# Moving 48 additions from GpSimd to VectorE's read of PSUM, and 36 key casts from VectorE to ScalarE, in an attention and mixer kernel

## Chip, cores, metric

One Trainium2 chip, one core. The metric is device time in microseconds (us). Medians are quoted with their range and number of runs. A ratio is the mean time of one kernel's fast runs over that of the other's of the same rounds, so it is not quite the ratio of the quoted medians; its 95% interval stands in brackets. "Faster" or "slower" means by over 2%.

## The reference

```python
# q, k, v: (B=8, H=8, S=1024, D=64); E, F: (64, 1024)
k_proj = einsum('ks,bhsd->bhkd', E, k);  v_proj = einsum('ks,bhsd->bhkd', F, v)
attn = softmax(q @ k_proj^T / sqrt(D));  x = (attn @ v_proj), heads joined   # (8, 1024, 512)
h = maximum(x^T @ w_tok1, 0) @ w_tok2                  # 1024 -> 256 -> 1024
u = x + h^T
out = u + maximum(u @ w_ch1, 0) @ w_ch2                # 512 -> 1536 -> 512
```

The last line is what the change touches: the sum of u and the down-projection's result.

## The kernel before

A small planner in the kernel puts every engine's instructions into one fixed order, from estimated durations; so changing an instruction's engine also changes TensorE's order. Up- and down-projection use a seven-product scheme (as in Strassen's), with sums of blocks on VectorE. The bf16 sums of this scheme (S and G below) have both inputs in SBUF:

```python
def s_sums(j):                       # four sums of 128x512 bf16 before the up-projection ("S", L677)
    one(0, a21, a22, add=True);  one(2, a11, a21)
    one(1, St[:, 0], a11, deps=(0,));  one(3, a12, St[:, 1], deps=(1,))
...
# at the end of up_set: four sums of 128x512 bf16 before the down-projection ("G", L842)
total(3, g21, G[:, 2, cs], True, [q21, g(2)]);  total(5, G[:, 0, cs], g21, False, [q21, g(0)])
total(4, G[:, 3, cs], G[:, 0, cs], False, [g(3), g(0)]);  total(6, G[:, 1, cs], G[:, 4, cs], False, [g(1), g(4)])
```

The down-projection, one of 16 blocks. Banks x, y, z collect products. Before the change ScalarE copies a bank to SBUF and GpSimd adds u there:

```python
def copy_add(dst, key, src, sh, dh):
    act(512, lambda: nc.scalar.copy(out=dst, in_=view(src)), writes=[key], uses=[bk[src]])
    pool(512, lambda: nc.gpsimd.tensor_add(out=dst, in0=dst, in1=u_of(sh, dh)),
         reads=u_key(sh), writes=[key])

product(1, 0)
act(512, lambda: nc.scalar.copy(out=view("y"), in_=view("x")), takes=[bk["y"]], uses=[bk["x"]])
product(7, 1); product(6, 2)
copy_add(db, "db", "y", 1, 0)
product(2, 3)
copy_add(o_of(0, 0), o_key(0, 0), "x", 0, 0)
product(5, 4)
dve(512, lambda: nc.vector.tensor_add(out=da, in0=view("y"), in1=u_of(1, 1)), ...)
dve(512, lambda: nc.vector.tensor_add(out=o_of(1, 1), in0=view("z"), in1=da), ...)
product(3, 5)
copy_add(o_of(0, 1), o_key(0, 1), "y", 0, 1)
store(0)
product(4, 6)
dve(512, lambda: nc.vector.tensor_add(out=o_of(1, 0), in0=view("z"), in1=db), ...)
store(1)
```

Loads and DMA transposes take turns by explicit dependencies. This becomes important below:

```python
def load_kv(b):                                   # k and v of one batch, issued by GpSimd
    last = load_group(b, "kv", turned_u.get((b - 2, 0)))   # behind an older u transpose
    if (b - 2, 1) in turned_u:
        tie(turned_u[b - 2, 1], last)
```

The softmax here doesn't subtract the row's maximum and nothing guards it: scores larger than these inputs give would overflow.

## Time and profile before

| | us |
|---|---|
| time, median of the runs before the prediction | 442.85 (441.47 to 443.28, 3 runs) |
| time of the profiled execution | 440.64 |
| span of the profile | 438.8 |
| TensorE busy, 50 to 400 us | 341.1 of 350 |

The second row is one to keep in mind: the profiled execution was faster than each of the timed runs. The prediction shows the engine line, the stretches, the longest stop and the groups. One part that it only mentions is the end. This is the timeline of the profile before (start, duration in us, engine, line, operation; in brackets the idle time before it and what ended that):

```profile
431.77 1.47 PE L902 MATMUL ps<-wT,G 128*128 128x256 bf16 x12
...
432.63 1.15 POOL L936 TENSOR_TENSOR o<-o,u 128x512 f32<-128x512 f32 x1 [2.89 <-ACT o L934]
433.35 0.69 DVE L964 TENSOR_TENSOR o<-ps,db 128x512 f32<-128x512 f32 x1 [2.16 <-PE ps L902]
433.81 0.84 SPq L929 DMA_DIRECT2D out_dram<-o  x2
```

Read it from below: both last stores (x2) are issued together at 433.81, because the first of them waits for a GpSimd add that lasts to 433.78, although the other half of what it stores was ready by 428.63.

### The profile page before, as it was taken

The page shows a single profiled execution, that of the slowest core. Times are in us where ns is not written, and L with a number is a line of the kernel's source. Part 1 is how long each engine was busy: PE and PEld are TensorE (multiplying, and loading weights), DVE is VectorE, ACT ScalarE, POOL GpSimd, SP SyncE. Part 2 cuts the span into 40 slices and gives each one's busy share as a digit, 9 for nine tenths or more (in the row PEclk, how much of TensorE's full clock was granted, in tenths as well). Part 3 has the DMA queues.
Part 4 walks back from the last instruction along what each step waited for, and adds up shares of the span by engine and source line. Part 5 has one row for each costly group of instructions (what it writes and reads, how often), then busy time and mean ns, then how long its engine had stood idle before and what let it go on. Part 6 is the DMA issues. An engine that isn't in the chain of part 4 may idle for free.

```text
span 438.8 us, 9331 instructions
## 1 busy us (share of the span) xinstructions
PE 417.0 (95%) x3726; PEld 336.1 (77%) x3754; DVE 323.8 (74%) x782; ACT 242.2 (55%) x440; POOL 124.7 (28%) x152
## 2 busy tenths in 40 slices
PE   7899999999999999999999899999999999999993
PEld 3587888576787778787878778787778878888883
DVE  2579969578788868888688868879687876867451
ACT  2758784275456544665457544575447653555530
POOL 8543243150142321422142310523212120223222
PEclk9999999999999999999999999999999999999998
DMA  9999999569799786978339894397830403151122
GB/s 166 207 200 206 206 206 220 97 105 228 132 149 197 167 167 140 175 185 151 120 54 208 160 154 143 61 237 125 179 74 19 128 0 121 26 145 45 53 97 96
DMA packets 89515, 60.89 MB, mean 139 GB/s; under 512 B 55680, under 2 KB 84864, under 8 KB 89472
## 3 DMA queue, kind: packets, MB, share of 16 engines
q0 software_dynamic: 34944, 45.09, 51.7%
q1 hardware_dynamic: 54448, 14.95, 19.8%
q8 instruction: 29, 0.48, 0.4%
q10 hardware_dynamic: 80, 0.26, 0.3%
q14 instruction: 14, 0.11, 0.1%
HBM read 59.24 MB, written 16.78 MB: 173 GB/s over the span
## 4 chain that ended last, share of the span: by engine, by line
PE 74%; DVE 12%; DMA 9%; ACT 2%; issue 1%; POOL 0%; DVEq 0%; ACTq 0%
PE ps L902 27%; PE ps L807 25%; DMA v_sb<-in_v_dram 6%; PE ps L617 5%; PE ps L637 5%; DVE S L677 3%; PE ps L465 3%; DMA uT<-u 3%; PE ps L586 2%; DVE G L842 2%; PE ps L563 2%; PE ps L387 2%; DVE x_sb L603 2%; DVE g L788 1%; DVE u L648 1%
## 5 line engine op out<-in xcount | busy, mean ns | idle before, releaser
L902 PEld LDWEIGHTS <-G 128*128 128x128 bf16 x1344 | 130.2, 98 | 26.6 <-issue 4.4
L902 PE MATMUL ps<-wc_sb,G 128*128 128x256 bf16 x768 | 104.1, 273 | 2.4 <-DVE da L952 1.6
L829 ACT ACTIVATE G<-ps 128x512 bf16<-128x512 f32 x96 | 57.4, 600 | 58.5 <-PE ps L807 58.3
L807 PEld LDWEIGHTS <-wc_sb 128*128 128x128 bf16 x768 | 73.1, 98 | 15.3 <-issue 2.0
L902 PE MATMUL ps<-wT,G 128*128 128x256 bf16 x576 | 78.2, 273 | 1.0 <-DVE o L956 1.0
L936 POOL TENSOR_TENSOR o<-o,u 128x512 f32<-128x512 f32 x32 | 39.1, 1221 | 102.9 <-ACT o L934 98.3
L807 PEld LDWEIGHTS <-wT 128*128 128x128 bf16 x576 | 55.2, 98 | 15.3 <-issue 4.3
L807 PE MATMUL ps<-S,wc_sb 128*128 128x256 bf16 x384 | 57.6, 273 | 0.3
L807 PE MATMUL ps<-uT,wc_sb 128*128 128x256 bf16 x384 | 57.6, 273 | 0.1
L807 PE MATMUL ps<-S,wT 128*128 128x256 bf16 x384 | 55.6, 273 | 0.2 <-DVE S L677 0.2
L788 DVE CUSTOM_DVE_ANT_0 g<-ps,ub 128x512 bf16<-128x512 f32 x48 | 32.7, 682 | 24.9 <-PE ps L807 24.8
L603 DVE TENSOR_TENSOR x_sb<-ps,rdn 128x256 bf16<-128x256 f32 x128 | 50.4, 416 | 0.5
L842 DVE TENSOR_TENSOR G<-G 128x512 bf16<-128x512 bf16 x96 | 45.4, 476 | 3.4 <-DVE G L842 0.5
L936 POOL TENSOR_TENSOR db<-db,u 128x512 f32<-128x512 f32 x16 | 18.7, 1166 | 98.9 <-ACT db L934 98.9
L648 DVE TENSOR_TENSOR u<-ps,x_sb 128x512 bf16<-128x512 f32 x56 | 37.9, 686 | 10.6 <-PE ps L637 6.7
L788 DVE CUSTOM_DVE_ANT_0 G<-ps,ua 128x512 bf16<-128x512 f32 x48 | 32.9, 686 | 14.0 <-ACT ua L835 12.9
L572 ACT ACTIVATE a<-ps 128x512 bf16<-128x512 f32 x64 | 37.3, 603 | 10.1 <-PE ps L563 9.1
L835 ACT COPY ua<-ps 128x512 f32<-128x512 f32 x48 | 28.2, 587 | 21.5 <-PE ps L807 20.8
L835 ACT COPY ub<-ps 128x512 f32<-128x512 f32 x48 | 28.1, 586 | 10.1 <-PE ps L807 10.1
L807 PE MATMUL ps<-uT,wT 128*128 128x256 bf16 x192 | 28.8, 272 | 3.4 <-DVE G L788 3.1
L586 PE MATMUL ps<-vb,a 128*128 128x130 bf16 x256 | 30.1, 220 | 1.5 <-DVE x_sb L603 1.1
L934 ACT COPY o<-ps 128x512 f32<-128x512 f32 x32 | 18.8, 587 | 21.6 <-PE ps L902 21.3
(70 smaller groups left out, 548.9 us busy)
## 6 DMA issues: line engine op xcount, KB each, us to landing
out_dram<-o POOLq DMA_DIRECT2D x30, 512.0 KB, 4.9
k_sb<-in_k_dram POOLq DMA_DIRECT2D x14, 512.0 KB, 7.5
v_sb<-in_v_dram POOLq DMA_DIRECT2D x14, 512.0 KB, 11.9
q_sb<-in_q_dram POOLq DMA_DIRECT2D x14, 512.0 KB, 7.7
wc_sb<-in_moe_w_ch_dram POOLq DMA_DIRECT2D x6, 256.0 KB, 12.4
wc_sb<-in_moe_w_ch_dram POOLq DMA_DIRECT2D x4, 384.0 KB, 12.6
k_sb<-in_k_dram POOLq DMA_DIRECT2D x4, 256.0 KB, 6.8
v_sb<-in_v_dram POOLq DMA_DIRECT2D x4, 256.0 KB, 7.4
```

Of the source, the lines that this page charges most:

```text
L572: lambda: nc.scalar.activation(out=a_t[h % 4], in_=bank(bk), func=ACT.Exp, scale=scale),
L586: nc.tensor.matmul(view()[:, 2 * jj : 2 * jj + 2].rearrange("p c d -> p (c d)"), a_t[h % 4][:, j * P : (j + 1) * P], vb[:, h].rearrange("k ...
L603: lambda: nc.vector.tensor_tensor(out=x_sb[:, 4 * half : 4 * half + 4, h * D : (h + 1) * D], in0=view()[:, :, 0:D], in1=rdn[:, :, None].to ...
L617: nc.tensor.matmul(bank(bk), wt1_sb[:, si, t * P : (t + 1) * P], x_sb[:, si, :], start=(si == 0), stop=(si == NSI - 1),)
L648: lambda: nc.vector.tensor_add(out=u_t[b % 2][:, si, :], in0=bank(bk), in1=x_sb[:, si, :]),
L788: nc.vector._custom_dve(TENSOR_ADD_SAT, out=out, in0=in0, in1=in1, s0=FMAX, s1=0.0)
L807: nc.tensor.matmul(t[:, c, :], w1_of(n, dd, 2 * m + c), a_of(j, n, dd), start=(n in (1, 7) and c == 0 and dd == 0), stop=(c == 1 and dd == 1),
L829: lambda: nc.scalar.activation(out=G[:, n, cs], in_=view(src), func=ACT.Relu),
L835: 512, lambda: nc.scalar.copy(out=dst, in_=view("y")), writes=[(name, s % 2)],
L842: 512, lambda: f(out=G[:, n, cs], in0=in0, in1=in1), ps=False, reads=deps,
L902: nc.tensor.matmul(view(X_OF[n])[:, t, :], G[:, G_OF[n], cc, t * P : (t + 1) * P], w2_of(n, cc), start=(n in (1, 7) and t == 0 and cc == 0 ...
L936: 512, lambda: nc.gpsimd.tensor_add(out=dst, in0=dst, in1=u_of(sh, dh)),
```

## The change

The intent: GpSimd adds nothing any more; VectorE adds u in the pass in which it reads PSUM anyway. In exchange ScalarE, relieved of 48 copies, takes VectorE's casts of the projected and turned keys. The diff, cut to its core:

```diff
-            lambda: nc.vector.tensor_copy(out=kp[:, hs, 0, :], in_=view()[0:KP, 0:hn]),
-            lambda: nc.vector.tensor_copy(out=kp[:, hs, 1, :], in_=view()[0:KP, 0:hn]),
+            lambda: nc.scalar.copy(out=kp[:, hs, 0, :], in_=view()[0:KP, 0:hn]),
+            lambda: nc.scalar.copy(out=kp[:, hs, 1, :], in_=view()[0:KP, 0:hn]),
 ...
-        dve(
-            hn * KP, lambda: nc.vector.tensor_copy(out=kT[0:D, hs, 0, :], in_=view()[0:D, 0:hn]),
+        act(
+            hn * KP, lambda: nc.scalar.copy(out=kT[0:D, hs, 0, :], in_=view()[0:D, 0:hn]),
 ...
-        def copy_add(dst, key, src, sh, dh):
-            act(512, lambda: nc.scalar.copy(out=dst, in_=view(src)), writes=[key], uses=[bk[src]])
-            pool(
-                512, lambda: nc.gpsimd.tensor_add(out=dst, in0=dst, in1=u_of(sh, dh)),
-                reads=u_key(sh), writes=[key],
+        def add_u(dst, key, src, sh, dh):
+            dve(
+                512, lambda: nc.vector.tensor_add(out=dst, in0=view(src), in1=u_of(sh, dh)),
+                reads=u_key(sh), writes=[key], uses=[bk[src]],
             )
 ... (the three calls of copy_add become calls of add_u)
```

More of the change, by code (lines that the diff above doesn't have):

```diff
@@ L307, in act @@
         return pl.add("ACT", t, t + 0.105, fn, **kw)
-    def pool(cols, fn, **kw):
-        t = cols / 512 * 1.15
-        return pl.add("POOL", t, t, fn, **kw)
     def sp(t, fn, **kw):
@@ L486, in kv_proj @@
         ]
-        dve(cols, e[0], writes=[("kp", 0, h) for h in heads], uses=[bk])
-        dve(cols, e[1], writes=[("kp", 1, h) for h in heads], uses=[bk])
+        act(cols, e[0], writes=[("kp", 0, h) for h in heads], uses=[bk])
+        act(cols, e[1], writes=[("kp", 1, h) for h in heads], uses=[bk])
         act(cols, e[2], writes=[("vb", 1, h) for h in heads], uses=[bk])
@@ L946, in down_block @@
         product(6, 2)
-        copy_add(db, "db", "y", 1, 0)
+        add_u(db, "db", "y", 1, 0)
         product(2, 3)
-        copy_add(o_of(0, 0), o_key(0, 0), "x", 0, 0)
+        add_u(o_of(0, 0), o_key(0, 0), "x", 0, 0)
         product(5, 4)
@@ L959, in down_block @@
         product(3, 5)
-        copy_add(o_of(0, 1), o_key(0, 1), "y", 0, 1)
+        add_u(o_of(0, 1), o_key(0, 1), "y", 0, 1)
         store(0)
```

## The prediction

> **What bounds the kernel now.** I read the engine line of the page first, then a table of busy time by stretches of 50 us, then the timeline where TensorE stops, then the groups by shape, then the waits.
>
> The page's engine line (busy us, share of the span, instructions):
>
> ```profile
> PE 417.0 (95%) x3726; PEld 336.1 (77%) x3754; DVE 323.8 (74%) x782; ACT 242.2 (55%) x440; POOL 124.7 (28%) x152
> ```
>
> The table by stretches (us, then busy time and count of PE, PEld, DVE, ACT, POOL):
>
> ```profile
> 100.00:150.00 50.00, 47.91 (x414) 38.09 (x415) 41.45 (x102) 29.13 (x54) 11.76 (x14) 1.00 0.99 181
> 200.00:250.00 50.00, 49.79 (x438) 40.50 (x440) 38.43 (x94) 28.59 (x53) 12.68 (x16) 1.00 0.69 134
> 250.00:300.00 50.00, 47.40 (x409) 38.01 (x411) 38.59 (x89) 27.02 (x49) 11.90 (x14) 1.00 0.80 147
> ```
>
> TensorE is the bound. Busy time alone would not prove it, but the timeline has groups of six 256-column matmuls that follow each other after 0.65 us, 0.108 us each, so the stream is dense and not just overlapping. From 50 to 400 us it is busy 341.1 us of 350. The change touches no matmul of the computation, so it can only win from the remaining 8.9 us there, and from start and end. That is already a ceiling: 442.85 - 8.9 = 434, which is a gain of 2.0%.
>
> Where TensorE stops is therefore the whole question. The longest stop is at 250 us, and the timeline around it (start, us, engine, line) shows the cause:
>
> ```profile
> 248.65 3.40 DVE L677 TENSOR_TENSOR S<-uT 128x512 bf16<-128x512 bf16 x1
> ...
> 249.47 1.18 POOL L936 TENSOR_TENSOR db<-db,u 128x512 f32<-128x512 f32 x1
> ...
> 250.59 1.16 POOL L936 TENSOR_TENSOR o<-o,u 128x512 f32<-128x512 f32 x1
> 251.97 0.68 DVE L788 CUSTOM_DVE_ANT_0 G<-ps,ua 128x512 bf16<-128x512 f32 x1
> ...
> 252.70 0.49 PE L807 MATMUL ps<-uT,wT 128*128 128x256 bf16 x3 [2.37 <-DVE G L788]
> ```
>
> One VectorE subtraction takes 3.40 us and ends 0.29 us after the second GpSimd add ends. [...] the next reader of PSUM (L788) starts only then, and TensorE sits 2.37 us. What the same instruction costs undisturbed is in the groups by shape (count, busy us, mean ns):
>
> ```profile
> L842 DVE TENSOR_TENSOR G<-G 128x512 bf16<-128x512 bf16 x96 | 45.4, 476 | 3.4 <-DVE G L842 0.5
> L842 DVE TENSOR_TENSOR G<-G,g 128x512 bf16<-128x512 bf16 x48 | 20.0, 416 | 0.1
> L677 DVE TENSOR_TENSOR S<-uT 128x512 bf16<-128x512 bf16 x32 | 16.2, 535 | 2.4 <-DMA uT<-u 2.4
> L648 DVE TENSOR_TENSOR u<-ps,x_sb 128x512 bf16<-128x512 f32 x56 | 37.9, 686 | 10.6 <-PE ps L637 6.7 <-PE ps L807 3.6
> L936 POOL TENSOR_TENSOR o<-o,u 128x512 f32<-128x512 f32 x32 | 39.1, 1221 | 102.9 <-ACT o L934 98.3 <-DMA uT<-u 4.5
> L936 POOL TENSOR_TENSOR db<-db,u 128x512 f32<-128x512 f32 x16 | 18.7, 1166 | 98.9 <-ACT db L934 98.9
> ```
>
> I went through all 256 bf16 sums of L677 and L842 in the trace. Sixteen take over 500 ns, every one overlaps a GpSimd add, and they end about 0.3 us after one; together they are 14.0 us longer than 16 x 0.417. The 60 that overlap only GpSimd's issue of a DMA average 415 ns, the 163 that overlap neither 417: no effect of the issues. L648, with one input in PSUM, shows none either (686 ns, longest 693).
>
> [...] the trace has 686 ns for 512 columns, and the new adds have this form. [...] The trace shows the turns for the projected keys and values:
>
> ```profile
> ACT vb L485 <- DVE kp L480: 10.5, 8, 2.0
> DVE kp L481 <- ACT vb L485: 3.7, 8, 0.7
> ```
>
> **The change part by part.**
> - GpSimd: 48 adds go, 39.1 + 18.7 = 57.8 us; 124.7 becomes 66.9, all of it DMA issue and start-up. [...]
> - ScalarE: the 48 copies go, 18.8 + 9.4 = 28.2 us. In come the key casts at the durations of its own value casts: 18 of 64x512 at 0.587, 6 of 64x256 at 0.372, 12 of 64x128 at 0.263: 10.6 + 2.2 + 3.2 = 16.0. 242.2 - 28.2 + 16.0 = 230.
> - VectorE: in come 48 adds of PSUM + u (one SBUF input) at 0.686, 32.9 us. Out go the key casts, 12.0 (kp) + 5.9 (kT) = 17.9, and the 14.0 of held time. 323.8 + 32.9 - 17.9 - 14.0 = 324.8: the load is unchanged, but without pieces of 1 to 3.4 us that nothing planned for.
> - TensorE's path: the stops that follow a held sum are 0.68 at 134.8 us, 0.31 at 146.4, 0.75 at 180.6, 0.36 at 199.0, 2.37 at 252.7 and 0.82 at 305.6, in all 5.3 us. They go: **-5.3**. The other three named stops between 50 and 400 us are 0.23, 0.95 (a VectorE reader behind four u sums and a key cast, at 90.3) and 0.94 (the v load, at 106.6). That load is issued behind a GpSimd add that itself was held to 2.22 us; without it it goes out 1 to 2 us sooner. I count half: **-0.5**.
> - Costs. The static order of TensorE's instructions gains two filler matmuls in the start-up, where the plan expects idle: five took 1.19 us, so **+0.5**. There ScalarE takes 12 more short casts in a phase in which it is on the chain of waits (exps and query copies), but two handoffs of some 0.3 us per head pair vanish; I call it even. New waits of TensorE on VectorE's reads of PSUM: the existing read of the same kind, da, held TensorE in mid-run once in 15 blocks (0.75, behind a held sum), so its undisturbed rate is nil; with three times as many such reads I allow **+1.0**. The last block keeps its two stops (0.72 on db, 0.85 on da): the order is the same, and 0.69 on VectorE stands where 0.59 on ScalarE stood.
> - Sum: 442.85 - 5.3 - 0.5 + 0.5 + 1.0 = **438.5 us**.
>
> **The rivals.**
> (a) VectorE becomes the late engine. It is at 83% in the stretch from 100 to 150 us and each such stretch takes six more adds, 4.1 us, that stand between two products into the same bank, where ScalarE read promptly before. If each of 16 blocks then stopped TensorE by 0.75 us as at 180.6, that is +12 - 5.3, about 449. Against it: three key casts (2.0 us) and 1.8 us of held time leave the same stretch, and VectorE's own idle waits for TensorE (24.8 us at L788) show slack.
> (b) Nothing moves: TensorE's stops close, and reordered work opens as many; 442 to 443. For it: a fifth of TensorE's instructions change place in the static order. Against it: stops without a held sum are rare now, 2.1 us in 350.
> (c) The start-up gets longer by the ScalarE casts: 12 x 0.26 = 3.2 us on the chain at worst, giving 441.5 with the rest as above. For it: ScalarE waits little between 10 and 30 us. Against it: only half of those casts stand before the exps, and the wait for VectorE's casts goes.
> (d) All of the mid-run idle goes and loads come sooner: 434 to 435. It needs every stop closed and none opened.
>
> **Range and chances.** The main term is 5.3 us with its cause seen in each case, so a gain is likely; (b) and (c) pull up, (d) down. 8 in 10: 435 to 443. Faster by over 2% needs below 434.0, beyond the ceiling of the mid-run idle: 0.04. Slower by over 2% needs (a) at more than its price, above 451.7: 0.03. Within 2%: 0.93.
>
> **What would show it.** Right: L677 and L842 at 410 to 420 ns in every group with none over 500; VectorE near 325 us busy, ScalarE near 230, GpSimd near 67; the new adds near 686 ns; TensorE's stop at 250 us gone, and named stops between 50 and 400 us of 2 to 3 us in place of 7.4. Wrong: bf16 sums still stretched[...]; stops of TensorE whose releaser is one of the new adds or a VectorE reader behind them, more than 3 us in all (rival a); first up-projections of the second batch over 1 us later than before (rival c); the same total of stops under other names (rival b).

## The result, and the profile after

| | before | after |
|---|---|---|
| time, median of 4 runs | 442.38 (441.47 to 443.28) | 431.83 (431.61 to 432.40) |
| profile: its own run / span | 440.64 / 438.8 | 431.61 / 429.8 |
| TensorE busy, 50 to 400 us | 341.1 | 347.6 |
| start of the last matmul to the end of the span | 5.87 | 4.70 |

The ratio is 0.9763 [0.9739, 0.9788]: **faster**, by 10.5 us, where 4.3 were predicted, and below the range.

Line numbers moved: L902 is now L898, L807 is L803, L842 is L838, L677 is L673, L788 is L784, L952 is L947, L964 is L959; the new adds are L931. The engine line of the page after:

```profile
PE 415.9 (97%) x3727; PEld 336.2 (78%) x3756; DVE 321.9 (75%) x794; ACT 231.1 (54%) x428; POOL 66.3 (15%) x104
```

The same stretches (us; then busy time and count of PE, PEld, DVE, ACT, POOL; granted clock, DMA share, GB/s) of the profile after:

```profile
100.00:150.00 50.00, 48.66 (x416) 38.75 (x419) 38.80 (x100) 27.20 (x50) 7.61 (x11) 1.00 0.89 157
200.00:250.00 50.00, 49.84 (x437) 40.69 (x440) 38.84 (x98) 27.66 (x49) 6.73 (x10) 1.00 0.81 148
250.00:300.00 50.00, 49.74 (x427) 39.73 (x431) 39.64 (x100) 27.04 (x48) 6.73 (x10) 1.00 0.81 151
```

The stretch from 250 us gained most: TensorE 49.74 in place of 47.40. The groups by shape (count, then busy us, mean ns of one, idle before) of the profile after:

```profile
L838 DVE TENSOR_TENSOR G<-G 128x512 bf16<-128x512 bf16 x96 | 39.8, 417 | 2.5
...
L673 DVE TENSOR_TENSOR S<-uT 128x512 bf16<-128x512 bf16 x32 | 12.4, 412 | 5.2 <-DMA uT<-u 5.2
...
L931 DVE TENSOR_TENSOR o<-ps,u 128x512 f32<-128x512 f32 x32 | 21.9, 685 | 10.2 <-PE ps L898 9.9
L931 DVE TENSOR_TENSOR db<-ps,u 128x512 f32<-128x512 f32 x16 | 10.8, 677 | 0.0
```

The means of 476 and 535 ns became 417 and 412; no bf16 sum takes over 427 ns.

Waits of TensorE on the new adds and on reads like them (total us, times, longest) in the profile after:

```profile
PE ps L898 <- DVE da L947: 1.5, 2, 0.8
...
PE ps L898 <- DVE db L931: 0.8, 1, 0.8
...
PE ps L582 <- DVE x_sb L599: 0.3, 1, 0.3
```

One `da` wait and the `db` wait lie in the last block. In mid-run there remain one `da` wait of 0.71 at 126.7 us and 0.34 at 145.9. The line `PE ps L807 <- DVE G L788: 3.1, 2, 2.4` of before has no counterpart. And the end:

```profile
423.93 1.47 PE L898 MATMUL ps<-wT,G 128*128 128x256 bf16 x12
424.13 0.69 DVE L931 TENSOR_TENSOR o<-ps,u 128x512 f32<-128x512 f32 x1 [0.83 <-PE ps L898]
424.85 1.65 SPq L925 DMA_DIRECT2D out_dram<-o  x2
425.44 0.69 DVE L959 TENSOR_TENSOR o<-ps,db 128x512 f32<-128x512 f32 x1 [0.62 <-PE ps L898]
```

The first store now goes at 424.85, beside the last matmuls and before VectorE's last add; the second follows that add.

**Where the 10.55 us came from, by the traces.** The two profiled spans differ by 9.0: 6.4 more TensorE busy time between 50 and 400 us, 0.2 in the first 50 us, 1.2 in the tail. The rest, 1.2, is less busy time over the same number of matmul records (3726 and 3727), and most likely belongs to the stops as well: pool_fill below, which has the order of before and as many records, is 1.1 us less busy too. Matched one by one, seven matmuls make up that difference. In before each of them starts behind a stop or a short pause (at 134.8, 146.4, 199.0, 252.7, 253.4, 305.6 and 351.7 us) and adds 0.16 us more busy time than in pool_fill, where it overlaps the matmul in front. So in these traces, whose matmul ends are modelled, such a stop costs 0.16 us beyond its idle time. For after, whose order differs, this matching was not possible. The other 1.5 is not in these two profiles: the profiled run of before was 1.74 faster than its median, that of after 0.22 faster than its own.

### The profile page after: what moved, and what is told of

It is laid out like the page before. It is cut to its first block, busy times and chain, and to the rows that moved or that the text cites. A ratio compares the mean times of both kernels' runs of the same rounds, so it can differ in the third digit from the quotient of the medians.

```text
span 429.8 us, 9229 instructions
## 1 busy us (share of the span) xinstructions
PE 415.9 (97%) x3727; PEld 336.2 (78%) x3756; DVE 321.9 (75%) x794; ACT 231.1 (54%) x428; POOL 66.3 (15%) x104
## 4 chain that ended last, share of the span: by engine, by line
PE 86%; DMA 6%; DVE 4%; ACT 2%; issue 1%; DVEq 0%
PE ps L898 31%; PE ps L803 31%; PE ps L613 6%; PE ps L633 4%; DMA v_sb<-in_v_dram 3%; PE ps L582 3%; DMA uT<-u 3%; PE ps L461 3%; PE ps L559 3%; PE ps L383 1%; DVE u L644 1%; PE ps L691 1%; PE ps L718 1%; PE ps L543 1%; ACT qT L551 1%
## 5 line engine op out<-in xcount | busy, mean ns | idle before, releaser
L898 PEld LDWEIGHTS <-G 128*128 128x128 bf16 x1344 | 129.9, 98 | 25.1 <-issue 2.8
L898 PE MATMUL ps<-wc_sb,G 128*128 128x256 bf16 x768 | 104.1, 273 | 2.3 <-DVE da L947 1.5
L803 PEld LDWEIGHTS <-wc_sb 128*128 128x128 bf16 x768 | 73.2, 98 | 16.3 <-issue 2.4
L898 PE MATMUL ps<-wT,G 128*128 128x256 bf16 x576 | 78.2, 273 | 0.0
L803 PEld LDWEIGHTS <-wT 128*128 128x128 bf16 x576 | 55.2, 98 | 12.3 <-issue 1.2
L803 PE MATMUL ps<-S,wc_sb 128*128 128x256 bf16 x384 | 57.7, 273 | 0.3
L803 PE MATMUL ps<-uT,wc_sb 128*128 128x256 bf16 x384 | 57.8, 273 | 0.1
L803 PE MATMUL ps<-S,wT 128*128 128x256 bf16 x384 | 55.7, 273 | 0.4 <-DVE S L673 0.4
L784 DVE CUSTOM_DVE_ANT_0 g<-ps,ub 128x512 bf16<-128x512 f32 x48 | 32.8, 682 | 29.3 <-PE ps L803 29.3
L925 POOL DMA_DIRECT2D out_dram<-o x30 | 16.4, 545 | 192.8 <-DVE o L931 130.8
L838 DVE TENSOR_TENSOR G<-G 128x512 bf16<-128x512 bf16 x96 | 39.8, 417 | 2.5
L784 DVE CUSTOM_DVE_ANT_0 G<-ps,ua 128x512 bf16<-128x512 f32 x48 | 32.8, 683 | 8.2 <-ACT ua L831 7.7
L844 ACT COPY ps<-ps 128x512 f32<-128x512 f32 x48 | 27.7, 577 | 17.1 <-DVE o L931 7.6
L594 DVE RECIPROCAL rdn<-ps 128x4 f32<-128x4 f32 x128 | 20.7, 173 | 18.0 <-PE ps L582 14.4
L582 PE MATMUL ps<-vb,a 128*128 128x130 bf16 x256 | 31.5, 220 | 0.4 <-DVE x_sb L599 0.3
L633 PE MATMUL ps<-hT_sb,wt_sb 128*128 128x512 bf16 x99 | 29.9, 379 | 0.4
```

The costliest lines, as they stand in the source:

```text
L582: nc.tensor.matmul(view()[:, 2 * jj : 2 * jj + 2].rearrange("p c d -> p (c d)"), a_t[h % 4][:, j * P : (j + 1) * P], vb[:, h].rearrange("k ...
L633: nc.tensor.matmul(bank(bk), wt2_sb[:, t, si::NSI], hT_sb[:, t, :], start=(t == 0), stop=(t == TC - 1),)
L784: nc.vector._custom_dve(TENSOR_ADD_SAT, out=out, in0=in0, in1=in1, s0=FMAX, s1=0.0)
L803: nc.tensor.matmul(t[:, c, :], w1_of(n, dd, 2 * m + c), a_of(j, n, dd), start=(n in (1, 7) and c == 0 and dd == 0), stop=(c == 1 and dd == 1),
L838: 512, lambda: f(out=G[:, n, cs], in0=in0, in1=in1), ps=False, reads=deps,
L898: nc.tensor.matmul(view(X_OF[n])[:, t, :], G[:, G_OF[n], cc, t * P : (t + 1) * P], w2_of(n, cc), start=(n in (1, 7) and t == 0 and cc == 0 ...
```

## The experiments

Sixteen runs were made, four of them of the two kernels unedited, in five groups of rounds, each with its own runs of before, whose median was 442.6 to 443.3.

### First question: is it the holds, the order, the casts or the adds?

My theory (the lock theory of the expectations): GpSimd's adds, which read SBUF, hold VectorE's sums (up to 3402 ns in the profile before, where the median is 418), and that is most of the gain. The rivals: TensorE's new order; ScalarE's casts; the shorter path of the new adds.

**pool_fill**: before, with each GpSimd add replaced by two fills of the same tile. GpSimd only writes. The order of TensorE, VectorE and ScalarE and every wait stay. The result is wrong on purpose.

```diff
-            pool(
-                512, lambda: nc.gpsimd.tensor_add(out=dst, in0=dst, in1=u_of(sh, dh)),
-                reads=u_key(sh), writes=[key],
-            )
+            def fill():
+                for _ in range(2):
+                    nc.gpsimd.memset(dst, 0.0)
+
+            pool(512, fill, reads=u_key(sh), writes=[key])
```

> The kernel before with GpSimd's 48 adds replaced by two fills of the same tile each (wrong result on purpose: u is lost). The order of instructions on TensorE, VectorE and ScalarE is identical to before, and every wait on GpSimd stays; only GpSimd's reads of SBUF are gone. Lock theory (the adds hold VectorE's sums of two SBUF tensors): no such sum over 500 ns, VectorE some 14 us less busy, TensorE's stops at 250 and 305 us gone, time 432 to 437. Path theory (results come late over ScalarE and GpSimd, and loads and stores queue behind the adds): time within 2 us of before, 440 to 444. Order theory (the re-planned order of instructions is what is better): also 440 to 444.

Measured: 434.34 (434.18 to 434.72) against 442.81, ratio 0.9811 [0.9773, 0.9850]. The page's engine line and the groups of pool_fill:

```profile
PE 415.9 (96%) x3726; PEld 336.2 (78%) x3754; DVE 310.6 (72%) x782; ACT 241.9 (56%) x440; POOL 116.5 (27%) x200
...
L842 DVE TENSOR_TENSOR G<-G 128x512 bf16<-128x512 bf16 x96 | 39.9, 419 | 3.0
...
L677 DVE TENSOR_TENSOR S<-uT 128x512 bf16<-128x512 bf16 x32 | 12.4, 418 | 2.4 <-DMA uT<-u 2.2
```

GpSimd is nearly as busy as before (116.5 against 124.7 us), ScalarE's copies are all there, and still the sums are at 418 ns and the time falls by **8.5 us**. So it is not GpSimd's load, nor ScalarE's copies, nor the order: it is GpSimd's *reads* of SBUF beside VectorE's sums of two SBUF tiles. GpSimd still writes there for about as long (two fills of 525 to 529 ns, where an add took 1.15 us), and every group of these sums averages 418 to 421 ns. L648, with one input in PSUM, takes 686 ns in both. The 8.5 us are four fifths of the gain by the medians (some 6.6 to 10 us by the interval of the ratio), and more than the 5.3 that I had read from the stops. The spread goes with it: 0.5 us over these runs, where before spread over 6.3.

**idle_adds**: the reverse. After, with a GpSimd add that nobody needs behind each new VectorE add.

```diff
+    scratch = tile_of([P, 2, DH], F32, "scratch")
-            dve(
-                512, lambda: nc.vector.tensor_add(out=dst, in0=view(src), in1=u_of(sh, dh)),
-                reads=u_key(sh), writes=[key], uses=[bk[src]],
-            )
+            def both():
+                nc.vector.tensor_add(out=dst, in0=view(src), in1=u_of(sh, dh))
+                nc.gpsimd.tensor_add(out=scratch, in0=dst, in1=u_of(sh, dh))
+
+            dve(512, both, reads=u_key(sh), writes=[key], uses=[bk[src]])
```

> The changed kernel with 48 GpSimd adds that nothing uses: after each of the new VectorE adds GpSimd adds u to its result into a scratch tile. Order on TensorE, VectorE and ScalarE identical to the changed kernel. Lock theory: sums of two SBUF tensors are held up again, 10 to 20 of them over 500 ns, and the time goes back by 5 to 10 us, to 437 to 442. Order or path theory: nothing waits for these adds but the loads and stores queued behind them, so 431 to 434.

Measured: 434.33 (434.22 to 435.21), only 2.5 over after. The S group and TensorE's longest mid-run wait:

```profile
L674 DVE TENSOR_TENSOR S<-uT 128x512 bf16<-128x512 bf16 x32 | 16.4, 538 | 2.0 <-DMA uT<-u 2.0
```

```profile
PE ps L804 <- DVE S L674: 2.2, 2, 1.8
```

The holds are back (17 sums, 11.2 us in all, the longest 2.23), and with them stops. But four fifths of the held time of before (14.0), which there costs 8.5 us, cost 2.5 in after's order. My figure of 5 to 10 was a miss: **the held time is not the cost**. The cost depends on which sums are held and what stands behind them. So "four fifths" holds for the way from before only: the same kind of reads is worth 8.5 us in the old order and 2.5 in the new one.

**casts_only** and **adds_only**: each half of the change alone; the edits are the upper and the lower half of the diff above.

> The other half: ScalarE takes the key casts, ScalarE and GpSimd still copy and add in the down-projection. Lock theory: the held sums stay, time 438 to 443. If the casts themselves (fewer handoffs between two readers of one bank) are worth something: 434 to 438. Lighter VectorE, so held sums may cost less than in the kernel before.

Measured: 441.81 (438.47 to 445.53, 20 runs, two of them over 1.5% above the fastest and left out of the ratio), ratio 0.9962 [0.9936, 0.9988]. The casts alone gain 0.4%. Seventeen sums are held in it, 18.8 us in all against 14.0 in before, so this run does not price the casts apart from the holds.

> Half of the change: VectorE adds u, the key casts stay on VectorE. VectorE then has 18 us more work than the changed kernel (about 340 us busy). Lock theory with slack on VectorE: most of the gain stays, 431 to 436. If VectorE's load matters (the casts were moved to make room for it): 436 to 442.

Measured: 440.02, 441.02, 443.24 and once 433.32. The record marks the first three as slow, as they lie over 1.5% above the fastest, and gives no verdict. No sum is held in the profile, which is of the 440.02 run, and yet it is nearly as slow as before. The trace names a wait of another kind: TensorE stops for 6.5 us at 138 us because the transposed queries are not there, a DMA, and behind the stop matmuls are slower: four of 256 columns that take 0.60 us at 137.83 take 1.06 at 145.28. The mean granted clock of this run is 0.992. That was on no list of mine; the third question takes it up.

### Second question: why 8.5 and not 5.3, and what is the tail worth?

**before_a, before_b, before_c, after_again**: the two kernels again without edits, for more profiles.

> The kernel before, unedited, for a second profile: its runs spread over 440.5 to 446.7 us while the kernels without GpSimd adds spread by under 1 us. Theory of variable holds: the length of held sums and the stops behind them differ from the first profile (14.0 us held, 5.3 us of stops), and the time follows the stops. Rival: the held sums are the same and the spread has another cause, for example a transpose or load that takes longer.

> The kernel before once more, for a third profile. The second profile (443.6 us) had two things that the first (440.64 us) lacked: a second hold of over 3 us (at 302 us) and a stretch of 3.4 us in which TensorE's clock was halved, right after the stop of 2.4 us at 250 us. Theory: the run time of the kernel before follows these, about 1.1 us for the second long hold and 1.7 us for a halved stretch; so a run near 440.5 shows neither, one near 442 one of them, one near 443.5 or more both. Rival: the profiles differ in time without differing in these.

> The kernel before, a fourth profile; as for the third: about 440.5 with neither, 442 with one, 443.5 or more with both a second long hold and a halved stretch.

> The changed kernel unedited, as the base for the two runs beside it, and a second profile of it. 431 to 433 us. If its first profile was typical, no bf16 sum over 500 ns and stops of TensorE from 50 to 400 us of about 2 us again.

| profile of before | its run | holds over 3 us | half-clock stretches in mid-run | mean granted clock |
|---|---|---|---|---|
| the one I predicted from | 440.64 | 1 | 0 | 0.997 |
| before_c | 440.74 | 1 | 0 | 0.997 |
| before_b | 442.11 | 1 | 1 | 0.993 |
| before_a | 443.60 | 2 | 1 | 0.992 |

The last two profiles came out as I had written down. The time of before rises with what I had seen only in its mildest form. Stops and clock in before_a's timeline, then its stretch of 2 us (granted clock third from the end):

```profile
252.70 0.60 PE L807 MATMUL ps<-uT,wT 128*128 128x256 bf16 x4 [2.40 <-DVE G L788]
...
254.41 1.06 PE L807 MATMUL ps<-uT,wc_sb 128*128 128x256 bf16 x4
...
302.25 3.27 DVE L677 TENSOR_TENSOR S<-uT 128x512 bf16<-128x512 bf16 x1
...
306.18 0.60 PE L807 MATMUL ps<-uT,wT 128*128 128x256 bf16 x4 [1.95 <-DVE G L788]
```

```profile
254.00:256.00 2.00, 2.00 (x12) 1.45 (x10) 1.78 (x6) 0.50 (x1) 0.00 (x0) 0.50 0.95 157
```

A group of four matmuls that takes 0.60 us takes 1.06 at 254.41: from 253.96 on TensorE was granted half its clock for 3.41 us (0.50 from 254 to 256 us, 0.66 from 256 to 258), which costs about 1.7, half of that time, by my estimate. The stop before it lasted 2.40. At 302 us a second sum is held over 3 us, and the stop there is 1.95 in place of 0.82. So some runs of before pay, beyond my 5.3, 1.7 for the clock, 1.1 for the second stop, or both. How many pay the first can be read from the mean granted clock on record for each run: 0.997 in the two profiles without a halved stretch in mid-run, 0.992 and 0.993 in the two with one; the lower clock at the end (0.78 over the last 5.5 us of the first profile, 0.96 from 400 us on in before_a) takes off 0.003 and 0.004 there. Of the 51 timed runs of before beside the experiments, 42 are at 0.995 or less (median 443.0 us), three at 0.996 (441.1 to 444.4) and only six at 0.997 (median 440.5). The profile that I predicted from is of the rare kind.

What decides whether half clock follows a stop was not shown. The stop at 250 us lasted 2.37 us in the first profile, and the granted clock stayed at 1.00 from 250 to 260 us; it lasted 2.40 in before_a, and the clock went to 0.50. In adds_again (third question) the clock averaged 0.68 from 140 to 144 us, within a stop of 6.27, and 0.50 from 144 to 148, as the matmuls start again. No run varied the length or the place of a stop alone.

after_again measured 431.66 (430.87 to 432.21), again without a held sum and with 0.3 us of named stops in mid-run.

**half_fill**: before, with the 32 adds on `o` replaced by fills and the 16 on `db` kept. I thought that only those sums are costly that wait for two GpSimd adds in a row, as at 248.65 in the prediction.

```diff
+            ... (fill as in pool_fill; add is the tensor_add of before)
+            pool(512, add if key == "db" else fill, reads=u_key(sh), writes=[key])
```

> The kernel before with 32 of the 48 GpSimd adds (those to o) replaced by fills that read nothing, the 16 adds to db kept (wrong result on purpose). Same order of instructions on TensorE, VectorE and ScalarE as before. If the costly holds are those in which two adds follow each other without a pause (db, then o), so that a sum waits for both: no hold over 1.8 us, no stop over 1.5 us at 250 us, no halved clock, and most of the 8.5 us that the version with fills alone gained: 434.5 to 437. If every held sum costs its own length: 16 of 48 adds left, a third of the loss, 437 or more.

Measured: 439.31 (436.85 to 440.44) against 443.26, ratio 0.9867 [0.9787, 0.9947]. The timeline of half_fill:

```profile
248.42 1.51 POOL L324 DMA_DIRECT2D q_sb<-in_q_dram  x2 [10.41 <-issue]
249.11 2.29 DVE L677 TENSOR_TENSOR S<-uT 128x512 bf16<-128x512 bf16 x1
249.94 1.18 POOL L940 TENSOR_TENSOR db<-db,u 128x512 f32<-128x512 f32 x1
...
252.06 0.60 PE L807 MATMUL ps<-uT,wT 128*128 128x256 bf16 x4 [1.54 <-DVE G L788]
```

That theory falls. A single add holds the sum for 2.29 us, and the sum stands still 0.83 us before the add's recorded start, behind GpSimd's issue of a load; the stop is 1.54. A third of the adds keeps a good part of the cost. How much is unclear: 4.5 of 8.5 us by the medians (439.31 against pool_fill's 434.34, less the 0.45 by which before itself was slower in these rounds), 2.5 by the ratios, as before scattered in these rounds up to 448.12. Ten sums are held here in all, 6.8 us together.

**tail_back**: after, with only the last block's last quarter by ScalarE's copy and GpSimd's add again. **quarter_stores**: after, with the last block's two stores of 512 KB split into four of 256 KB.

```diff
+            if j == NSB - 1 and (sh, dh) == (0, 1):
+                act(512, lambda: nc.scalar.copy(out=dst, in_=view(src)), writes=[key], uses=[bk[src]])
+                pl.add("POOL", 1.15, 1.15,
+                    lambda: nc.gpsimd.tensor_add(out=dst, in0=dst, in1=u_of(sh, dh)), ...)
+                return
```

> The changed kernel, but in the last block the last quarter (output o of the first rows, second half of the columns) goes over a ScalarE copy and a GpSimd add again. In the profile before, the first of the two last stores waited for that GpSimd add and both stores were issued together at 433.8 us. Tail theory: the last matmul-to-end time goes from 4.7 back to 5.7 to 5.9 us and the run is 0.9 to 1.3 us slower than the changed kernel. If the shorter tail of the changed kernel had another cause: no difference over 0.3 us.

> A try at a better version: the changed kernel with the four quarters of the last block stored each as soon as it is ready (four stores of 256 KB in place of two of 512 KB), so that only 256 KB are left after the last add. If the tail is set by the bytes still to write: 0.4 to 0.8 us faster than the changed kernel. If it is set by the fixed time of one store: no difference[...].

tail_back: 433.25 (431.83 to 433.54), 1.6 over after_again of the same rounds by the medians, 1.4 by the means, 0.5 by the profiled executions; from the start of the last matmul to the end 6.1 us in place of 4.7. Its timeline has before's picture back, both stores at once:

```profile
423.63 1.15 POOL L934 TENSOR_TENSOR o<-o,u 128x512 f32<-128x512 f32 x1 [9.54 <-ACT o L931]
...
424.81 0.83 SPq L925 DMA_DIRECT2D out_dram<-o  x2
```

quarter_stores: 431.45 (431.25 to 431.69), no difference. So the tail is worth some 1.4 us, and it comes from when the first store goes. That a smaller last store gains nothing is shown only together with its rows of 1 KB in place of 2 KB.

### Third question: why do the adds without the casts fail?

**adds_again**: adds_only once more.

> The half of the change that leaves the key casts on VectorE, run again because its first four runs lay apart (433.3, and 440.0 to 443.2) and its profile showed one query transpose overtaken by loads, with a stop of 6.6 us at 138 us. Theory: two outcomes of one race between a transpose and the loads, 433 to 434 without the collision and 440 to 443 with it, in a mixture again. Rival: the first session was at fault, and all runs lie near 433 now.

Measured: 440.24, 440.42, 434.53, 441.52: the same mixture, so it is no accident of one group of rounds. Nor are the slow runs only a label: the mean granted clock on record is 0.986 to 0.992 in the six slow runs of adds_only and adds_again, 0.998 and 1.000 in the two fast ones, of which no trace was kept. The timelines of DMA issues (the durations are those of the issuing instructions) and TensorE in adds_again:

```profile
119.97 12.89 SPq L524 DMA_TRANSPOSE qT<-q_sb  x2
...
121.87 1.48 POOL L320 DMA_DIRECT2D k_sb<-in_k_dram  x2 [9.15 <-PE ps L803]
...
144.74 0.61 PE L559 MATMUL ps<-qT,kT 128*128 128x512 bf16 x1 [6.27 <-DMA qT<-q_sb]
```

While the two query transposes run, GpSimd issues the next k and v loads. The first transpose lands 4.9 us after its issue; the second, issued at 121.77, lands at 144.69, after 22.9 us and 1.0 us behind the last of the loads. In after_again the query load goes out at 106.88, here at 111.21, as the first u transpose starts at 81.5 and at 85.8. Theory: the casts help only because without them this load and these transposes meet. Rival: VectorE is too full with adds and casts.

**adds_tied** and **after_tied**: the k and v loads wait for the query transposes, *in place of* the older u transpose.

```diff
+        turned_q[b] = j                      # in q_transpose
 ...
-        last = load_group(b, "kv", turned_u.get((b - 2, 0)))
+        last = load_group(b, "kv", turned_q.get(b - 1) or turned_u.get((b - 2, 0)))
```

> The half with the key casts on VectorE, and the loads of keys and values of the next batch made to wait for the query transposes of this batch (they waited for an older transpose). TensorE's order is planned anew with that dependency, so about a sixth of its instructions change place. Theory: the 440 us of six of eight runs of that half come from loads that overtake a query transpose; then all runs lie at 431.5 to 434.5 and no stop over 2 us is left from 50 to 400 us. If the casts cost this time on VectorE: 438 to 441 still.

> The changed kernel with the same dependency, as a try at a better version and a control. Its trace shows no such collision, so no difference over 1 us from 431.7; if it is over 1 us slower, the dependency has a cost of its own that also bears on the run beside it.

adds_tied: 447.67 (447.19 to 447.85), ratio 1.0107: 1.1% over before, which counts as the same by the 2% rule, and 7 us over adds_again. My edit had taken a dependency away: the loads now went out at 82.27, into the u transposes that start at 85.74:

```profile
PE ps L805 <- DMA uT<-u: 9.0, 1, 9.0
```

So the run does not tell the theories apart, except that it is a second case of a load in flight beside a transpose: the first u transpose landed 17.4 us after its issue (4.4 in after_tied, where it was issued before the loads), and TensorE stood 9.0 us. after_tied, with the same edit: 429.71 (429.67 to 430.51), ratio 0.9709 [0.9689, 0.9730]. I had expected no difference over 1 us from 431.7, so this is a miss. TensorE is busy 350.0 of the 350 us from 50 to 400, but 349.6 in after_again, so that does not explain the 2 us, and their cause stays open. **It is the fastest version of this study**, and it beats both kernels; that the edit helps one order and harms the other shows how little of this is general.

**adds_both** and **after_both**: the loads wait for both.

```diff
     def load_kv(b):
+        n0 = len(pl.jobs)
         last = load_group(b, "kv", turned_u.get((b - 2, 0)))
+        if b - 1 in turned_q:
+            for j in pl.jobs[n0:]:
+                j.deps.add(turned_q[b - 1])
+            also[pl.jobs[n0]] = turned_q[b - 1]
+        ... (the entries of also become waits where the instructions are issued)
```

> The half with the key casts on VectorE again, where the key and value loads keep their old wait (an older transpose of u) and also wait for this batch's query transposes; adds_tied had replaced the old wait, and the loads then ran into a transpose of u (9 us stop). Theory: with both waits no transpose is overtaken and all runs lie at 431 to 434.5. If the casts on VectorE cost this time by VectorE's load: 438 to 441.

> The changed kernel with the same two waits: control, and a try at the best version; after_tied had 429.7. Expected 429 to 432.

adds_both: 432.47 (432.14 to 432.89) against 443.12, ratio 0.9749 [0.9719, 0.9780]. Its timeline and its engine line:

```profile
121.01 5.65 SPq L526 DMA_TRANSPOSE qT<-q_sb  x2
...
129.35 1.49 POOL L320 DMA_DIRECT2D k_sb<-in_k_dram  x2 [15.89 <-PE ps L498]
```

```profile
PE 418.2 (97%) x3754; PEld 336.0 (78%) x3754; DVE 338.5 (79%) x830; ACT 218.3 (51%) x392; POOL 66.3 (15%) x104
```

With the load held back to 129.35 both transposes land within 6.0 us of their issue, and no mid-run stop is over 0.7. VectorE carries adds and casts together, 338.5 us, and the time is back: the rival falls. (The new dependency also plans TensorE's order anew; no run separates that from the load's time, but the stop of 6.3 us behind the transpose is gone.) after_both: 431.42 (430.39 to 431.87), ratio 0.9725. Between the two the casts are worth about 1.0 us. In the plain adds_only their absence costs about 9, by the timing of a transfer.

## Why the prediction was wrong, step by step

- **Mechanism, right.** GpSimd's adds held VectorE's sums of two SBUF tiles (sixteen over 500 ns, up to 3402); without the adds they average 412 to 417 ns. pool_fill shows it with the order of all three engines unchanged. Two details: the prediction's 16, 60 and 163 sums make 239 of 256; the other 17 overlap a GpSimd add too, but started first or while the add itself was held, and average 418 ns. The new adds, with one input in PSUM, show no hold: 677 and 685 ns, where L648 took 686.
- **Busy times, right.** VectorE 321.9 us (324.8 predicted), ScalarE 231.1 (230), GpSimd 66.3 (66.9), the new adds 677 and 685 ns (686).

**The failed step** is the size of the term for the stops behind held sums, "They go: -5.3". The cause and the cases were right, the price was not: pool_fill, which takes away GpSimd's reads and leaves the order, measured 8.5 by the medians. The term has no place for half clock after the stop (1.7 us by the estimate above, in most runs of before by their granted clock), for a second hold over 3 us (1.1 in some), or for the restart behind a stop (0.16 each). The second failed step is the last block, put at 0: it measured 1.2 by the traces, 1.4 to 1.6 by tail_back. Term by term (us; negative is a gain):

| term, as predicted | predicted | measured | from |
|---|---|---|---|
| stops behind held sums, idle time in the profiled execution | -5.3 | -5.3 | the two traces: none of these stops is left |
| the three other named stops | -0.5 (v load only) | -2.1 | 0.23 + 0.95 + 0.94, all gone |
| new waits in mid-run | +1.0 | +1.05 | 0.71 on `da`, 0.34 on `x_sb` |
| start-up | +0.5 | -0.2 | 44.5 in place of 44.3 busy in 50 us |
| tail | 0 | -1.2 | the two traces; 1.4 to 1.6 by tail_back |
| less busy time of the same matmuls | 0 | -1.2 | the two traces; in pool_fill 1.1, restarts behind stops |
| profiled run against median run | 0 | -1.5 | 1.74 - 0.22 |
| sum | -4.3 | -10.45 (10.55 by the medians) | |

- **"-5.3" was read rightly and is still too small for the runs that are timed.** By the profiled executions pool_fill wins 440.64 - 434.72 = 5.9; by the medians 8.5. Most of the difference is where the profiled run lay in the spread that the holds make: before ran from 440.45 to 446.73 in pool_fill's rounds, pool_fill from 434.18 to 434.72. I took a stop from an execution at the fast end and subtracted it from the median of slower ones.
- **"The last block keeps its two stops": true, but the wrong question.** They are still 0.8 each. I asked what TensorE waits for there, not when the first store can go.
- **"+0.5" for two more fillers** was not borne out: the first 50 us are no worse.
- **"-0.5" for the v load.** I halved it out of caution and took the other two stops as staying. In pool_fill the v load's stop is still there, 1.6, so it is not due to the holds; in the whole change it is gone.
- **"A ceiling: 434".** Its own sentence names start and end as well, and then leaves them out. It took the idle time between 50 and 400 us of one execution for all that could be won. Tail, granted clock and the spread between runs lie outside it. This put "faster" at 0.04.
- **The rivals.** (a), (b) and (c) did not occur. (d), 434 to 435, came nearest, and lacked the tail, the clock and the spread too. A rival that I did not have, a load that runs into transposes, is what the half-change adds_only showed; the whole change avoids it by its timing, not by design.

The runs split the gain in another way: from 442.81 to 434.34 is the holds, 8.5; from there to 431.7, 2.6 us, of which the tail is 1.4 to 1.6 and the v load up to 1.6, each measured singly and not quite additive.

**What stays open.** Why four fifths of the held time cost 2.5 us in one order, where all of it costs 8.5 in the other, I can only describe: in before's order two holds stand ahead of a PSUM reader that the up-projection waits for, in idle_adds the longest stop is 1.8, and the mean granted clock of its four runs is 0.998 to 1.000, where before_a with its halved stretch has 0.992. I did no run that moves single holds. Nor does a run show what decides, from execution to execution, whether the second hold at 302 us grows beyond 3 us; in before_a that sum starts 0.69 us ahead of the first of two adds and waits for both, in the other profiles 0.77 us behind it.

## What to carry to other kernels

Where VectorE adds or subtracts two SBUF tiles ahead of a PSUM reader that TensorE waits for, keep GpSimd from reading SBUF beside it: give the add to the engine that reads PSUM anyway. Here GpSimd's reads cost 8.5 us in one order (pool_fill) and 2.5 in another (idle_adds). Before a term is sized from stops, compare the profiled run with the timed runs, in time and in granted clock, and if they differ take further profiles; a ceiling from idle time in the middle holds for that execution only, and without its tail. And when an engine that also issues loads is relieved, or the order changes, check where the loads now land: tying them explicitly behind the transposes that they disturb was worth 8 us in one order here, and tying them wrongly cost 7.

## Further figures from these traces

- The held sum ended 0.3 us after the recorded end of the last GpSimd add beside it: in before 252.05 against 251.75, in before_a 252.04 against 251.75 and 305.52 against 305.23, in half_fill 251.40 against 251.12. It began 0.8 us before the recorded start of the first add, while GpSimd was issuing a load for 1.51 us (before: 248.65 against 249.47; half_fill: 249.11 against 249.94). Sums that stood through two adds in a row took 3.40 us (before), 3.41 and 3.27 (before_a).
- A query transpose landed 22.9 us after its issue with k and v loads issued beside it (adds_again), and within 6.0 us with them held back (adds_both).
